# Attention and expert layers on one core: nine of sixteen head pairs keep their probabilities as fp16 halves, turned by DMA

## The chip, the cores and the metric

The kernel runs on one core of a Trainium2 chip. The metric is the device time of one execution in microseconds (us). The engines are TensorE (PE), VectorE (DVE), ScalarE (ACT), GpSimd (POOL) and SyncE (SP), which here only issues DMAs. Each engine takes its own instructions in the order in which they stand in its queue; semaphores join the queues.

## The reference

Attention with queries averaged in pairs, over 4 batches of 8 heads with 1152 keys of 64 numbers, and then a two-layer network on the joined heads:

```python
q_pool = q.reshape(B, H, S // 2, 2, D).mean(axis=3)      # 576 queries per head
scores = scale * np.matmul(q_pool, k.transpose(0, 1, 3, 2))
scores = scores - np.max(scores, axis=-1, keepdims=True)
attn = np.exp(scores)
attn = attn / (np.sum(attn, axis=-1, keepdims=True) + 1e-09)
attn_out = np.matmul(attn, v)
x = attn_out.transpose(0, 2, 1, 3).reshape(B * S, H * D)  # 2304 x 512
h = x @ w_in                                              # 512 -> 2048
g = np.where(h > 0.0, h, np.exp(np.minimum(h, 0.0)) - 1.0)
return g @ w_out                                          # 2048 -> 512
```

## The kernel before, in words

**Units.** A batch is a unit; its 8 heads are 4 head pairs. A pair has 9 steps: four tiles of 128 queries for each head and one step in which the last 64 queries of both heads share the 128 partitions. So a batch has 36 steps and the program 144.

**A step** (`attention`, from L744): `scores` (L761, L766, L773) makes 128x1152 scores in three PSUM banks, the only buffer `s`, out of fp16 halves of query and key; `biggest` (L779, DVE) scales them into an SBUF buffer `ep` (fp32, four buffers) and takes the extreme of each row; `expo` (L785, ACT) writes the exponentials in place with their sum; `recip` (L790, L791, DVE) makes 1/sum; `norm_pool` (L794, POOL; sometimes L797 on DVE) multiplies `ep` by it. Then PE turns the nine 128x128 blocks of `ep` (L820, fp32, into PSUM `r`, three to a buffer) and ACT (L832) or DVE (L835) copies each three into `pT` (fp32). When both heads of a tile are turned, `pv` (L851) multiplies by the values: 18 fp32 matmuls, one head in the first 64 columns of the array and the other in the last 64, into one `r` buffer, which DVE (L863) or ACT (L860) copies to `x32`.

**Before a pair** (`prep`, from L477): SP loads q, k and v; q and k are scaled by a power of two and split into fp16 halves (L492 and L504 or POOL); two DMA transposes (`qT` L571, nine blocks; `kT` L583, eighteen blocks) and three small copies on SP make the operands of `scores`. v stays fp32.

**The network** (`experts`, from L874): for each batch, in two groups of 256 and 320 tokens, 16 first-layer tasks (M1, L949; 24 matmuls of 256 columns or 12 of 320) with activation work on ACT, POOL and DVE (L963 to L1002), and the second layer (M2, L1021) in tasks of 12 matmuls of 512 columns. The last 64 tokens of a batch take 48 matmuls in column halves. Weights are decoded, scaled and split at the start (L645 to L700).

**The order** is set when the program is built. `Plan.run` (L114) plays the program through with a duration for every task and gives an engine, whenever it is free, the ready task with the smallest key whose buffers are free. Keys come from `CFG` (L19) and the position of a step. `weave` (L153) puts the transposes of a step between the matmuls of an M1 or M2 task, one for one.

Of the kernel before, what the change touches and what calls it, by code (L numbers as in the profile page):

```python
# [19 lines left out]
    LOADS=-114467, WI0=33877, WIT=9245, WO0=755935, WOT=6543, T0=2082, T1=1393, M0=16194,  # L20
    M1=49670, KS=15309, KM=4108, KE=81609, KH=27848, KL=992, KV=-2143, KN=220, KX=-18520,
    KO=-10657, PEN=-570, W0L=-16875, WIN=726, PD=18136, KS0=34876, KM0=13622, KE0=132045,
    KH0=40116, KL0=31322, KV0=2811, KX0=-445, PLM0=0, NS0=36, PLM=0, M2=10343, DP=0, FK=0,
    PENW=-3339, PENH=-2500, FL=2000, PH0=2, PH=1, KT=-33611, KT0=390, LV=16680, HW=3136,
    PENN=1577, PENT=23, PLP=1, WLP=1, HIP=0, PA=-2820, PB=-5460,
)

# [21 lines left out]
class Task:  # L49
    def __init__(self, eng, dur, key, emit, after, bufs):  # L50
        self.eng, self.dur, self.key, self.emit = eng, dur, key, emit
        self.ways = {eng: (dur, emit)}
        self.after = [a for a in after if a is not None]
        self.bufs = bufs
        self.pen = None
        self.parts, self.thin, self.guests, self.modes = None, None, [], ("full", "full")
        self.kids, self.left, self.ready, self.end = [], 0, 0.0, None


class Plan:  # L60
# [5 lines left out]
    SWITCH, THIN = 94.0, 58.0  # L66
# [11 lines left out]
    def add(self, eng, dur, key, emit, after=(), bufs=(), ways=(), modes=None, parts=None, thin=None):  # L78
# [6 lines left out]
        t.parts, t.thin = parts, thin  # L85
        t.n = len(self.tasks)
        self.tasks.append(t)
        return t
# [25 lines left out]
    def run(self):  # L114
# [38 lines left out]
        def weave(t, need):  # L153
            hold = {x for x, _ in need}
            host, guests = (None, [(t, need)]) if t.thin else ((t, need), [])
            if host is None:
                for key, _, h in wait["PE"]:
                    if key > t.key + CFG["HW"]:
                        break
                    if h.parts:  # L160
                        got = self._slots_for(h, hold)
                        if got is not None:
                            host = (h, got)
                            hold |= {x for x, _ in got}
                            break
            if host is None:
                return t, need, []
            for key, _, g in wait["PE"]:
                if len(guests) >= len(host[0].parts) // 4:
                    break  # L170
                if g.thin and g is not t:
                    got = self._slots_for(g, hold)
                    if got is not None:
                        guests.append((g, got))
                        hold |= {x for x, _ in got}
            return (*host, guests)

        while done < len(self.tasks):
# [5 lines left out]
            while again:  # L184
                again = False
                for e in engines:
# [23 lines left out]
                    guests = []  # L210
                    if t.parts or t.thin:
                        t, need, guests = weave(t, need)
# [11 lines left out]
                    slow = 1.0 / self.COLD if cold else 1.0  # L224
                    for i, (g, got) in enumerate(guests):
                        self._take(got)
                        gone(g)
                        g.start = now
                        t.guests.append(g)
                        rest[e] += 3 * self.THIN  # L230
                        heapq.heappush(landing, (now + slow * 3 * (i + 1) * (self.THIN + t.dur / len(t.parts)), g.n, g))
                        done += 1
# [44 lines left out]
    def emit(self):  # L277
        for t in self.run():
            for o in [t, *t.guests]:
                for b in o.bufs:  # L280
                    if b.ap is None:
                        ap = self.make[b.tag](b.slot)
                        b.ap = ap if b.tag == b.tags[0] else self.lend[b.tags[0], b.tag](ap)
            if not t.guests:
                t.emit()
                continue
            thin = [f for g in t.guests for f in g.thin]
            for i, f in enumerate(t.parts):
                if i < len(thin):
                    thin[i]()  # L290
                f()
# [3 lines left out]
def attention_moe_kernel(  # L295
# [30 lines left out]
    pool("v32", 3, [128, 2, NCH, D], F32)  # L326
# [4 lines left out]
    pool("sm", 4, [128, 14], F32)  # L331
    pool("nm", 5, [128, 4], F32)
# [5 lines left out]
    pool("us", 3, [128, 16], F32)  # L338
# [3 lines left out]
    pool("tmp", 5, [128, 512], F32)  # L342
    plan.pool("wm", 1, lambda j: None)
    pool("xr", 1, [128, 8], F32)
# [59 lines left out]
    for u in units:  # L404
# [3 lines left out]
        for p in range(NP):  # L408
            pr = Rec()
            pr.u, pr.p, pr.i, pr.t0 = u, p, len(pairs), None  # L410
            pr.steps = []
# [25 lines left out]
    wk = sb.tile([128, 64], F32, name="wk")  # L437
    iwi, cwi, mf, nwi = (wk[:, j * NG:(j + 1) * NG] for j in range(4))
    mo = wk[:, 32:48]
    ck, so_w, wt = wk[:, 48:49], wk[:, 49:50], wk[:, 50:60]  # L440
# [16 lines left out]
    def across(src, n, key, after, bufs, take):  # L457
# [6 lines left out]
        def most():  # L464
            nc.vector.tensor_reduce(xr.ap[0:n, 0:1], xp.ap[0:n, 0:128], axis=AX.X, op=ALU.max)
            nc.vector.tensor_scalar(xr.ap[0:n, 4:4 + n], ident[0:n, 0:n], xr.ap[0:n, 0:1], None, op0=ALU.mult)

        def back():
            nc.tensor.matmul(xp.ap[:, 256:256 + n], ones[0:n].to_broadcast([n, 128]), xr.ap[0:n, 4:4 + n], start=True, stop=True)  # L469
# [7 lines left out]
    def prep(pr, t0, t1):  # L477
# [74 lines left out]
        nsum = 2  # L552
# [5 lines left out]
        sums.append(plan.add("ACT", act(1152) + 90.0, key[1], absum(k_h, k_s, 1), [tk], [kn, k32, sm]))  # L558

        def up(top):  # L560
# [4 lines left out]
            ts(nc.vector, a[:, 12:13], a[:, 0:1], a[:, 1:2], -1.0 / (2.0 * float(D) ** 0.5))  # L565

# [23 lines left out]
        kl = halves(1152, key[6], key[7], k_h, k_l, k_s, 1, [sc], [kn, k32, sm])  # L590
# [153 lines left out]
    def attention(st):  # L744
# [39 lines left out]
        def expo():  # L784
            nc.scalar.activation(  # L785
                out=e_(), in_=e_(), func=AF.Exp, bias=nm.ap[:, 0:1], scale=-1.0, accum_out=nm.ap[:, 2:3],
            )

        def recip():
            nc.vector.tensor_scalar(nm.ap[:, 3:4], nm.ap[:, 2:3], 1e-9, None, op0=ALU.add)  # L790
            nc.vector.reciprocal(nm.ap[:, 3:4], nm.ap[:, 3:4])  # L791

        def norm_pool():
            nc.gpsimd.tensor_scalar(e_(), e_(), nm.ap[:, 3:4], 1.0, op0=ALU.mult, op1=ALU.mult)  # L794

        def norm_dve():
            nc.vector.tensor_scalar(e_(), e_(), nm.ap[:, 3:4], None, op0=ALU.mult)  # L797

        def norm_act():
            nc.scalar.activation(out=e_(), in_=e_(), func=AF.Copy, scale=nm.ap[:, 3:4])  # L800
# [7 lines left out]
        th = plan.add("POOL", pol(S), t0 - K("KH", u), norm_pool, [tr], [ep, nm],  # L808
                      [("DVE", Port(760.0), norm_dve), ("ACT", act(S), norm_act)])
        th.pen = CFG["PENN"]  # L810

# [4 lines left out]
        for j in range(0, NCH, 3):  # L816
            tp = plan.buf("r")

            def one(c, j=j, tp=tp):
                nc.tensor.transpose(tp.ap[:, c * 128:(c + 1) * 128], e_()[:, (j + c) * 128:(j + c + 1) * 128], ident)  # L820

            thin = [lambda c=c, one=one: one(c) for c in range(3)]

            def turn(thin=thin):
                for f in thin:
                    f()

            def dst(j):
                return pT.ap[:, st.h or 0, j:j + 3].rearrange("p c s -> p (c s)")

            def out_act(j=j, tp=tp):
                nc.scalar.activation(out=dst(j), in_=tp.ap[:, 0:384], func=AF.Copy)  # L832

            def out_dve(j=j, tp=tp):
                nc.vector.tensor_copy(dst(j), tp.ap[:, 0:384])  # L835

            tt = plan.add("PE", 335.0, t0 - K("KT", u) + j, turn, [th], [ep, tp, pT], thin=thin)
            tq = plan.add("ACT", 410.0, t0 - K("KL", u) + j, out_act, [tt], [tp, pT], [("DVE", 480.0, out_dve)])
            tq.pen = CFG["PENT"]
            pr.pt.append(tq)  # L840
# [3 lines left out]
        x = plan.buf("r")  # L844

        def pv():
            for c in range(NCH):
                for h in range(2):
# [3 lines left out]
                        x.ap[64 * h:64 * h + 64, 0:n], pr.v32.ap[:, h, order[c]], p,  # L852
                        start=(c == 0), stop=(c == NCH - 1), skip_group_check=True,
                    )

# [3 lines left out]
        def xa():  # L859
            nc.scalar.activation(out=xdst(), in_=x.ap[:, 0:n], func=AF.Copy)  # L860

        def xb():
            nc.vector.tensor_copy(xdst(), x.ap[:, 0:n])  # L863

        tp = plan.add("PE", 18 * (2.0 * n / 2.4 + 2.5), t0 + K("KV", u), pv,
                      list(pr.pt) + pr.vdone, [x, pT, pr.v32], modes=("col", "col"))
        u.xdone[0 if st.t < 2 else 1].append(plan.add("DVE", 230.0, t0 + K("KV", u) - K("KX", u), xb, [tp], [x, u.x32],
# [6 lines left out]
    def experts(u, gi, t0, t1):  # L874
# [60 lines left out]
        if True:  # L935
# [3 lines left out]
            for g in range(NG):  # L939
                for f0 in range(0, 2, per):  # L940
# [15 lines left out]
                    p1 = [lambda f=f, i=i, m1=m1: m1(f, i) for f in range(per) for i in range(3 * KD)]  # L956

                    def m1_all(p1=p1):
# [133 lines left out]
```

## Time and profile before

| | us |
|---|---|
| median of 3 runs | 927.88 (924.21 to 932.52) |
| profiled execution, its own time | 928.17 |
| its span on the core | 926.4 |
| PE busy in the span | 855.7 |
| DVE, ACT, POOL busy | 598.2, 589.2, 390.6 |

The sum of the prediction is made against the profiled execution, 928.2 us, of which the span is 926.4 and 1.8 lies around it. A busy PE is counted from the start of a matmul to its modelled end, and matmuls overlap; so what one matmul costs is read from the distance between starts, or from the chain of work, not from its mean duration.

### The profile page before, as it was taken

To read this page: it belongs to the slowest core of one execution; us is meant where nothing else is said; L and a number is where in the kernel's file an instruction comes from. 1 tells how busy PE (TensorE), PEld (TensorE's weight loads), DVE (VectorE), ACT (ScalarE), POOL (GpSimd) and SP (SyncE) were. 2 spreads that over 40 slices of the span, in tenths; PEclk is the share of its full clock that TensorE was granted. 3 is DMA by queue.
4 is the path that set the end of the run, shared out by engine and by line. 5 is a ranking of instruction groups with operands and counts; after the bars stand their busy time and mean duration, and the time that the engine had idled before them with its cause. 6 is when DMAs were issued, how large, how long until landed. Compare 5 with 4: busy or idle time off the path is not lost.

```text
span 926.4 us, 19421 instructions
## 1 busy us (share of the span) xinstructions
PE 855.7 (92%) x7731; PEld 611.8 (66%) x7731; DVE 598.2 (65%) x1325; ACT 589.2 (64%) x1114; POOL 390.6 (42%) x387
## 2 busy tenths in 40 slices
PE   1268888899999999999999999999999999999997
PEld 0146656687577767776677766777677767777563
DVE  7898889998848765654477656654477646642350
ACT  4457888877757855756577755756578655553460
POOL 3455356378637742433255523343155523332120
PEclk9999999999999999999999999999999999999999
DMA  8963585600404520342151430323160200000000
GB/s 307 231 170 69 158 198 172 174 2 27 109 30 106 123 88 13 70 77 69 41 115 48 89 89 1 71 62 75 49 116 27 59 13 1 13 2 1 29 1 29
DMA packets 97691, 72.30 MB, mean 78 GB/s; under 512 B 59456, under 2 KB 77888, under 8 KB 97600
## 3 DMA queue, kind: packets, MB, share of 16 engines
q1 hardware_dynamic: 97600, 71.06, 30.7%
q8 instruction: 61, 1.00, 0.4%
q14 instruction: 30, 0.25, 0.1%
HBM read 45.09 MB, written 4.72 MB: 54 GB/s over the span
## 4 chain that ended last, share of the span: by engine, by line
PE 76%; DVE 12%; DMA 5%; ACT 3%; issue 2%; POOL 1%; SPq 1%; ACTq 0%; DVEq 0%; POOLq 0%
PE r L949 18%; PE r L1021 17%; PE r L820 14%; PE r L851 14%; PE s L761 7%; PE s L773 4%; DVE ep L779 3%; DMA kT<-kn 3%; DMA qT<-qn 2%; DVE tmp L646 1%; DVE g L649 1%; DVE tmp L645 1%; ACT ep L785 1%; PE s L766 1%; PE r L469 1%
## 5 line engine op out<-in xcount | busy, mean ns | idle before, releaser
L794 POOL TENSOR_SCALAR ep<-ep,nm 128x1152 f32<-128x1152 f32 x139 | 178.7, 1286 | 286.7 <-DVE nm L791 181.1
L820 PE MATMUL r<-ident,ep 128*128 128x128 f32 x1296 | 273.9, 282 | 6.0 <-ACT x L860 1.7
L779 DVE TENSOR_SCALAR_CACHE_REDUCE ep<-s,sm 128x1152 f32<-128x1152 f32 x144 | 203.6, 1414 | 76.9 <-PE r L820 47.0
L949 PE MATMUL r<-x,wi 128*128 128x256 f16 (+1 forms) x1536 | 242.0, 286 | 1.7 <-ACT x L860 1.6
L832 ACT ACTIVATE pT<-r 128x384 f32<-128x384 f32 x334 | 153.8, 489 | 121.2 <-PE r L820 119.3
L785 ACT ACTIVATE ep<-ep,nm 128x1152 f32<-128x1152 f32 x144 | 180.4, 1252 | 66.3 <-DVE ep L779 64.7
L820 PEld LDWEIGHTS r<-ident,ep 128*128 128x128 f32 x1296 | 166.5, 142 | 48.8 <-issue 30.0
L1021 PE MATMUL r<-wo,g 128*128 128x512 f16 (+1 forms) x792 | 180.5, 380 | 0.0
L949 PEld LDWEIGHTS <-wi 128*128 128x128 f16 x1536 | 153.0, 100 | 24.7 <-issue 0.8
L851 PE MATMUL r<-pT,v 128*64 128x128 f32 (+1 forms) x2880 | 160.0, 265 | 1.5 <-ACT pT L832 1.5
L851 PEld LDWEIGHTS r<-pT,v 128*64 128x64 f32 x2880 | 142.6, 137 | 20.4 <-issue 12.1
L761 PE MATMUL s<-kT,qT 128*128 128x512 f16 (+2 forms) x480 | 97.2, 334 | 17.6 <-DVE ep L779 16.8
L1021 PEld LDWEIGHTS <-g 128*128 128x128 f16 (+1 forms) x792 | 69.5, 102 | 62.7 <-issue 1.8
L971 POOL TENSOR_SCALAR tmp<-tmp,us 128x320 f32<-128x320 f32 (+1 forms) x96 | 60.5, 632 | 114.6 <-ACT tmp L966 111.5
L976 DVE SCALAR_TENSOR_TENSOR tmp<-r,wk,tmp 128x320 f32<-128x320 f32 (+1 forms) x96 | 58.2, 612 | 43.4 <-POOL tmp L971 43.0
L761 PEld LDWEIGHTS <-qT 128*128 128x128 f16 (+1 forms) x480 | 39.6, 101 | 54.7 <-issue 27.7
L963 ACT ACTIVATE tmp<-r 128x320 f32<-128x320 f32 (+1 forms) x96 | 46.5, 485 | 36.3 <-PE r L949 31.8
L835 DVE COPY pT<-r 128x384 f32<-128x384 f32 x98 | 53.7, 553 | 19.9 <-PE r L820 19.0
L966 ACT ACTIVATE tmp<-tmp,us 128x320 f32<-128x320 f32 (+1 forms) x96 | 58.6, 612 | 2.0
L773 PE MATMUL s<-kT,qT 64*128 64x512 f16 (+1 forms) x320 | 57.8, 398 | 0.0
L790 DVE TENSOR_SCALAR nm<-nm 128x1 f32<-128x1 f32 x144 | 21.4, 149 | 46.7 <-ACT ep L785 45.8
L1002 DVE TENSOR_TENSOR g<-tmp,g 128x320 f16<-128x320 f32 (+1 forms) x56 | 33.5, 604 | 19.7 <-ACT g L990 14.9
(111 smaller groups left out, 787.1 us busy)
## 6 DMA issues: line engine op xcount, KB each, us to landing
k<-in_k_dram SPq DMA_DIRECT2D x16, 576.0 KB, 4.7
v<-in_v_dram SPq DMA_DIRECT2D x16, 576.0 KB, 3.9
q<-in_q_dram SPq DMA_DIRECT2D x32, 256.0 KB, 3.3
qT<-qT SPq DMA_DIRECT2D x48, 144.0 KB, 2.9
g<-in_moe_w_in_dram SPq DMA_DIRECT2D x13, 512.0 KB, 5.2
g<-in_moe_w_out_dram SPq DMA_DIRECT2D x13, 512.0 KB, 4.3
out_dram<-tmp SPq DMA_DIRECT2D x16, 256.0 KB, 2.0
h<-in_moe_w_in_dram SPq DMA_DIRECT2D x3, 512.0 KB, 3.8
```

The lines of the kernel that those rows point to most:

```text
L761: nc.tensor.matmul(s.ap[rows, c, 0:n], pr.qT.ap[:, 0, j, rows], keys[h][c], start=True, stop=False, skip_group_check=True,)
L773: nc.tensor.matmul(s.ap[rows, c, 0:512], pr.qT.ap[r, 1, j, rows], keys[h][c][r], start=False, stop=True, skip_group_check=True,)
L779: nc.vector.tensor_scalar(e_(), s.ap.rearrange("p a b -> p (a b)")[:, 0:S], pr.sm.ap[:, 12:13], None, op0=ALU.mult, op1=ALU.min, accum_out ...
L785: nc.scalar.activation(out=e_(), in_=e_(), func=AF.Exp, bias=nm.ap[:, 0:1], scale=-1.0, accum_out=nm.ap[:, 2:3],)
L794: nc.gpsimd.tensor_scalar(e_(), e_(), nm.ap[:, 3:4], 1.0, op0=ALU.mult, op1=ALU.mult)
L820: nc.tensor.transpose(tp.ap[:, c * 128:(c + 1) * 128], e_()[:, (j + c) * 128:(j + c + 1) * 128], ident)
L832: nc.scalar.activation(out=dst(j), in_=tp.ap[:, 0:384], func=AF.Copy)
L851: nc.tensor.matmul(x.ap[64 * h:64 * h + 64, 0:n], pr.v32.ap[:, h, order[c]], p, start=(c == 0), stop=(c == NCH - 1), skip_group_check=True,)
L949: nc.tensor.matmul(hp.ap[:, f * n:(f + 1) * n], w_in16[g][:, a, c, (f0 + f) * 128:(f0 + f + 1) * 128], x16.ap[:, e, c, g0:g0 + n], start=( ...
L966: nc.scalar.activation(out=en.ap[:, :m], in_=en.ap[:, :m], func=AF.Exp, scale=us.ap[:, 8 + g:9 + g])
L971: nc.gpsimd.tensor_scalar(en.ap[:, :m], en.ap[:, :m], -1.0, us.ap[:, 5:6], op0=ALU.add, op1=ALU.mult)
L1021: nc.tensor.matmul(op.ap[r0:r0 + tn, :], gt[qd].ap[:, a, fi, o:o + tn], w_out16(f // 2)[:, e, f % 2, :], start=(i < 128 // tn), stop=(i >= ...
```

## The change

A table `SPLIT` marks nine head pairs, three in each of the batches 1 to 3; batch 0 stays as it was. For a marked pair v is split into two fp16 halves as well (`v16`), and its 81 steps go another way after `recip`: ACT or POOL writes the fp16 high half of the normalized probabilities into a new buffer `hb` (two of them), DVE writes the low half over `ep` (L793), and two DMA transposes on SP's queue (L799) turn both into `pT`. The values are multiplied in three terms (high x high, high x low, low x high) with 54 fp16 matmuls in column halves (L862), and the copy to `x32` takes the scale back. `weave` goes: the transposes that stay stand together. All keys of `CFG` are new. To make room, `v32` goes from 3 to 2 buffers, `tmp` from 5 to 4, `sm` from 4 to 3, `us` from 3 to 2, and `nm` and `xr` become columns of `wk`.

```diff
-    LOADS=-114467, WI0=33877, WIT=9245, WO0=755935, WOT=6543, T0=2082, T1=1393, M0=16194,
+    LOADS=-28648, WI0=-4682, WIT=8948, WO0=1686424, WOT=1874, T0=2082, T1=500, M0=16259,
...
+SPLIT = ("ffff", "ssfs", "ssfs", "ssfs")
...
-        def weave(t, need):
...
-    pool("v32", 3, [128, 2, NCH, D], F32)
+    pool("v32", 2, [128, 2, NCH, D], F32)
+    pool("v16", 1, [128, 2, NCH, 2, D], F16)
+    pool("hb", 2, [128, S], F16)
...
-    pool("sm", 4, [128, 14], F32)
-    pool("nm", 5, [128, 4], F32)
+    pool("sm", 3, [128, 14], F32)
+    plan.pool("nm", 5, lambda j: wk[:, 61 + 2 * j:63 + 2 * j])
...
+        if pr.split:
+            v16 = pr.v16 = plan.buf("v16")
+            v_s, v_h, v_l = (lambda: v32.ap), (lambda: v16.ap[:, :, :, 0]), (lambda: v16.ap[:, :, :, 1])
+            sums.append(plan.add("ACT", act(1152) + 90.0, key[2], absum(k_h, v_s, 2), [tv, sums[1]], [kn, v32, sm]))
...
-        pr.vdone = [tv]
+        pr.vdone = [halves(1152, key[11], key[12], v_h, v_l, v_s, 2, [sc], [v16, v32, sm])] if pr.split else [tv]
...
+        if pr.split:
+            hb = plan.buf("hb")
+            e16 = lambda: e_().bitcast(F16)[:, 0:S]
...
+            def phi():
+                nc.gpsimd.tensor_scalar(hb.ap, e_(), nm.ap[:, 1:2], 1.0, op0=ALU.mult, op1=ALU.mult)
+
+            def phi_act():
+                nc.scalar.activation(out=hb.ap, in_=e_(), func=AF.Copy, scale=nm.ap[:, 1:2])
+
+            def plo():
+                nc.vector.scalar_tensor_tensor(
+                    out=e16(), in0=e_(), scalar=nm.ap[:, 1:2], in1=hb.ap, op0=ALU.mult, op1=ALU.subtract
+                )
+
+            def ptr(j):
+                def f():
+                    nc.sync.dma_start_transpose(
+                        out=p16(j).rearrange("p (c s) -> p c s", c=NCH), in_=e16() if j else hb.ap
+                    )
+                return f
...
+            pr.pt.append(plan.add("DMA", Move(1400.0, 1100.0, True), t0 - CFG["KC"], ptr(0), [th], [hb, pT]))
+            pr.pt.append(plan.add("DMA", Move(1400.0, 1100.0, True), t0 - CFG["KC"], ptr(1), [tl], [ep, pT]))
...
+        def pv_split():
+            for j, (a, e) in enumerate(((0, 0), (0, 1), (1, 0))):
+                for c in range(NCH):
+                    for h in range(2):
...
+                        nc.tensor.matmul(
+                            half(h), pr.v16.ap[:, h, order[c], e], p,
+                            start=(j + c == 0), stop=(j == 2 and c == NCH - 1), skip_group_check=True,
+                        )
```

On PE before, in batch 2, the transposes of a step (L820, from `ep` into `r`) stand one for one between the matmuls of an M1 task (L949), and the fp32 product with the values (L851) follows:

```order
L820 MATMUL r1_5350<-ident_70,ep2_5043 128x128
L949 LDWEIGHTS wi0_61
L949 MATMUL r0_5348<-x160_4344,wi0_61 128x320
...
L949 MATMUL r0_5348<-x160_4344,wi0_61 128x320
L851 MATMUL r1_5384<-pT1_5152,v322_3869 64x128 x18
```

On PE after, at about the same place in batch 2, an M2 task (L1035) is followed by the fp16 product with the values of a marked pair (L862; 54 matmuls, each with a weight load of its own) and then by scores (L727):

```order
L1035 LDWEIGHTS g0_4873
L1035 MATMUL r0_5468<-wo2_1476,g0_4873 128x512
L862 LDWEIGHTS v160_5093
L862 MATMUL r2_5566<-pT0_5226,v160_5093 64x128
...
L862 MATMUL r2_5566<-pT0_5226,v160_5093 64x128
L727 LDWEIGHTS qT0_4520
L727 MATMUL s0_5623<-kT0_4495,qT0_4520 64x512
```

Nothing of the marked pair's probabilities passes PE any more before this product.

On DVE before, there, a step's row extreme (L779) stands among copies of transposes (L835) and joins of the network (L976):

```order
L779 TENSOR_SCALAR ep3_5465,nm1_5464<-s0_5412,sm2_3721 128x1152
L835 COPY pT0_5352<-r4_5469 128x384
L976 SCALAR_TENSOR_TENSOR tmp0_5488<-r0_5429,wk_69,tmp0_5488 128x320
L790 TENSOR_SCALAR nm1_5464<-nm1_5464 128x1
L791 RECIPROCAL nm1_5464<-nm1_5464 128x1
```

On DVE after, low halves (L793) of four steps stand ahead of the next row extreme (L745), whose buffer `ep0` is the one that the first of them wrote:

```order
L793 SCALAR_TENSOR_TENSOR ep0_5095<-ep0_5095,wk_69,hb0_5331 128x1152
L990 SCALAR_TENSOR_TENSOR tmp1_5385<-r4_5360,wk_69,tmp1_5385 128x320
L793 SCALAR_TENSOR_TENSOR ep2_5272<-ep2_5272,wk_69,hb1_5375 128x1152
L793 SCALAR_TENSOR_TENSOR ep3_5379<-ep3_5379,wk_69,hb0_5526 128x1152
L793 SCALAR_TENSOR_TENSOR ep1_5466<-ep1_5466,wk_69,hb1_5546 128x1152
L745 TENSOR_SCALAR ep0_5564,wk_69<-s0_5491,sm0_4070 128x1152
```

The row extreme now stands behind a low half and behind its transfer, which frees `ep0`.

On SP's queue after, there, high and low halves (L799, from `hb` and `ep` into `pT`) stand between the transposes and copies of a pair's operands (L537, L543, L546); before, it held no transposes but two for each pair:

```order
L537 DMA_TRANSPOSE qT0_5779<-qn0_5262 128x9x128
L1061 DMA out_0_dram<-tmp0_5668 128x512
L799 DMA_TRANSPOSE pT0_5859<-hb0_5772 128x9x128
L543 DMA qT0_5779<-qT0_5779 64x1152 x2
L799 DMA_TRANSPOSE pT0_5859<-ep1_5744 128x9x128
L799 DMA_TRANSPOSE pT0_5859<-hb1_5790 128x9x128
L546 DMA qT0_5779<-qT0_5779 64x1152
L799 DMA_TRANSPOSE pT0_5859<-ep3_5774 128x9x128
```

One queue serves loads, outputs, operand transposes and the 162 new ones, in this order.

## Rows read from the trace of the kernel before

**Rows 1.** The page: busy time of each engine; PE and DVE in 40 slices.

```profile
span 926.4 us, 19421 instructions
PE 855.7 (92%) x7731; PEld 611.8 (66%) x7731; DVE 598.2 (65%) x1325; ACT 589.2 (64%) x1114; POOL 390.6 (42%) x387
...
PE   1268888899999999999999999999999999999997
...
DVE  7898889998848765654477656654477646642350
```

**Rows 2.** The page: the chain that ended last, by engine and by line.

```profile
PE 76%; DVE 12%; DMA 5%; ACT 3%; issue 2%; POOL 1%; SPq 1%; ACTq 0%; DVEq 0%; POOLq 0%
PE r L949 18%; PE r L1021 17%; PE r L820 14%; PE r L851 14%; PE s L761 7%; PE s L773 4%; DVE ep L779 3%; DMA kT<-kn 3%; DMA qT<-qn 2%; DVE tmp L646 1%; DVE g L649 1%; DVE tmp L645 1%; ACT ep L785 1%; PE s L766 1%; PE r L469 1%
```

**Rows 3.** Busy time by window, cut where a batch's first L779 stands; batches 0 to 2.

```profile
core 0: us, PE busy (x) PEld busy (x) DVE busy (x) ACT busy (x) POOL busy (x), PEclk, DMA share, GB/s
0.00:198.00 198.00, 137.30 (x1321) 99.75 (x1322) 172.64 (x384) 141.36 (x288) 94.58 (x78) 0.99 0.65 173
198.00:406.00 208.00, 205.81 (x1872) 150.43 (x1870) 145.98 (x314) 143.42 (x263) 117.00 (x112) 1.00 0.28 66
406.00:617.00 211.00, 209.59 (x1928) 151.76 (x1927) 128.21 (x294) 136.10 (x252) 83.22 (x86) 1.00 0.28 66
```

**Rows 4.** The same view for three other windows.

```profile
60.00:182.00 122.00, 107.36 (x1117) 78.98 (x1116) 108.48 (x254) 100.85 (x210) 57.69 (x44) 0.99 0.59 154
198.00:820.00 622.00, 616.98 (x5670) 448.16 (x5668) 393.11 (x876) 407.07 (x749) 276.48 (x279) 1.00 0.25 59
...
182.00:240.00 58.00, 56.99 (x517) 42.36 (x517) 52.99 (x101) 45.30 (x84) 43.12 (x39) 1.00 0.13 33
```

**Rows 5.** The chain in order of time (start, us, what): transposes woven and alone.

```profile
423.12 0.11 PE r L820
423.23 0.21 PE r L1021
...
185.64 1.13 PE r L820 x9
```

**Rows 6.** The same chain: products with the values; a pair of column halves.

```profile
353.22 2.12 PE r L851 x36
...
493.69 1.20 PE r L851 x36
...
190.08 0.06 PE s L766 x2
```

**Rows 7.** Groups by line and shape: us in all, mean ns | idle before.

```profile
L785 ACT ACTIVATE ep<-ep,nm 128x1152 f32<-128x1152 f32 x144 | 180.4, 1252 | 66.3 <-DVE ep L779 64.7
L794 POOL TENSOR_SCALAR ep<-ep,nm 128x1152 f32<-128x1152 f32 x139 | 178.7, 1286 | 286.7 <-DVE nm L791 181.1 <-PE r L820 27.5 <-ACT tmp L1039 10.3
L832 ACT ACTIVATE pT<-r 128x384 f32<-128x384 f32 x334 | 153.8, 489 | 121.2 <-PE r L820 119.3
L835 DVE COPY pT<-r 128x384 f32<-128x384 f32 x98 | 53.7, 553 | 19.9 <-PE r L820 19.0
L976 DVE SCALAR_TENSOR_TENSOR tmp<-r,wk,tmp 128x320 f32<-128x320 f32 x64 | 34.3, 544 | 17.1 <-POOL tmp L971 16.7
L976 DVE SCALAR_TENSOR_TENSOR tmp<-r,wk,tmp 128x512 f32<-128x512 f32 x32 | 23.9, 747 | 26.3 <-POOL tmp L971 26.3
```

**Rows 8.** Source lines on DVE and SP: duration ns min/median/max; landing us.

```profile
L504 DVE SCALAR_TENSOR_TENSOR kn<-k,sm,kn x14: 810/832/1831, 408.9 to 717.8; 128x576 f16<-128x576 f32 x14
...
L571 SPq DMA_TRANSPOSE qT<-qn x16: 1283/1846/2481, 24.4 to 729.6; - x16
...
DMA to landing us min/median/max: 3.4/3.8/6.9
...
L583 SPq DMA_TRANSPOSE kT<-kn x16: 2492/4068/7399, 28.3 to 731.0; - x16
```

**Rows 9.** SP's queue in order of time: a plain issue.

```profile
409.33 0.51 SPq L529 DMA_DIRECT2D q<-in_q_dram  x1
```

More of the change, by code (lines that the diff above doesn't have):

```diff
@@ L151, in gone @@
                 wait[o].remove((t.key, t.n, t))
-        def weave(t, need):
[L154 to L176, printed above, removed]
         while done < len(self.tasks):
@@ L278, in emit @@
         for t in self.run():
[L279 to L291, printed above, removed]
+            for b in t.bufs:
+                if b.ap is None:
+                    ap = self.make[b.tag](b.slot)
+                    b.ap = ap if b.tag == b.tags[0] else self.lend[b.tags[0], b.tag](ap)
+            t.emit()
 @with_exitstack
@@ L815, in attention, with one, turn, dst @@
         pT = pr.pT
[L816 to L840, printed above, removed]
+        if pr.split:
+            hb = plan.buf("hb")
+            e16 = lambda: e_().bitcast(F16)[:, 0:S]
+            p16 = lambda j: pT.ap.bitcast(F16).rearrange("p h c s -> p (h c s)")[:, 2 * S * (st.h or 0) + j * S:][:, :S]
+            def phi():
[12 more added lines that the diff above has]
+                return f
+            hw = [("ACT", act(S), phi_act), ("POOL", pol(S), phi)]
+            th = plan.add(*hw[0][:2], t0 - CFG["KA"], hw[0][2], [tr], [ep, nm, hb], hw[1:])
+            tl = plan.add("DVE", dve(S), t0 - CFG["KB"], plo, [th], [ep, nm, hb])
+            pr.pt.append(plan.add("DMA", Move(1400.0, 1100.0, True), t0 - CFG["KC"], ptr(0), [th], [hb, pT]))
+            pr.pt.append(plan.add("DMA", Move(1400.0, 1100.0, True), t0 - CFG["KC"], ptr(1), [tl], [ep, pT]))
+        else:
+            th = plan.add("POOL", pol(S), t0 - K("KH", u), norm_pool, [tr], [ep, nm],
+                          [("DVE", Port(760.0), norm_dve), ("ACT", act(S), norm_act)])
+            th.pen = CFG["PENN"]
+            for j in range(0, NCH, 3):
+                tp = plan.buf("r")
+                def one(c, j=j, tp=tp):
+                    nc.tensor.transpose(tp.ap[:, c * 128:(c + 1) * 128], e_()[:, (j + c) * 128:(j + c + 1) * 128], ident)
+                def turn(one=one):
+                    for c in range(3):
+                        one(c)
+                def dst(j):
+                    return pT.ap[:, st.h or 0, j:j + 3].rearrange("p c s -> p (c s)")
+                def out_act(j=j, tp=tp):
+                    nc.scalar.activation(out=dst(j), in_=tp.ap[:, 0:384], func=AF.Copy)
+                def out_dve(j=j, tp=tp):
+                    nc.vector.tensor_copy(dst(j), tp.ap[:, 0:384])
+                tt = plan.add("PE", 335.0, t0 - K("KT", u) + j, turn, [th], [ep, tp, pT])
+                tq = plan.add("ACT", 410.0, t0 - K("KL", u) + j, out_act, [tt], [tp, pT], [("DVE", 480.0, out_dve)])
+                tq.pen = CFG["PENT"]
+                pr.pt.append(tq)
@@ L844, in attention, with half @@
         x = plan.buf("r")
+        def half(h):
+            return x.ap[64 * h:64 * h + 64, 0:n]
         def pv():
```

105 lines of the change are left out of this document (50 added, 55 removed).

## The prediction

> **What bounds the kernel now.** I read the page's busy shares and slices first, then the chain that ended last, then the busy time by window and at last single lines. The page shows one engine far ahead: PE is busy 92% of the span, DVE 65%, ACT 64%, and PE's slices are at nine tenths from the ninth on while DVE's fall from the twelfth on [rows 1]. The chain says the same: 76% of the span is PE, and of the lines on it the transposes (L820) and the products with the values (L851) have 14% each [rows 2]. The windows show where: in batch 0 PE is busy 137.3 of 198 us and DVE 172.6, so there DVE and the loads set the pace; in batches 1 and 2 PE is busy 205.8 of 208 and 209.6 of 211 us, DVE 146.0 and 128.2 [rows 3]. Over 198 to 820 PE is busy 99.2% (617.0 of 622), DVE 63%, ACT 65%, POOL 44%, at a granted clock of 1.00 [rows 4]. All marked steps lie after batch 0, so what PE saves is saved where PE is the bound, until another engine or queue takes its place.
>
> **PE's terms.** *Transposes.* A marked step loses nine of them; 81 steps make 729. Woven, a transpose holds the chain 0.11 us and the matmul beside it 0.21 [rows 5], so 729 x 0.11 = 80 us go. Of the transposes that stay, batch 0's mostly stand alone already; 27 unmarked steps of later batches lose the weaving, at 0.126 each alone (1.13 for nine) [rows 5]: 243 x 0.016 = +4 us.
>
> *Products with the values.* Nine pairs have 36 whole tiles and nine half ones. A whole fp32 tile takes 2.12 us [rows 6]. The fp16 form needs 54 matmuls of 128 columns, in 27 pairs of column halves. The trace has such a pair in the scores of the shared step: two matmuls of 128 columns in two column halves hold the chain 0.06 us [rows 6]. So 27 x 0.06 = 1.62 us, 0.50 less, and 36 x 0.50 = 18 us go. The bound above is the weight loads: in a half fp32 tile 36 loads and matmuls take 1.20 us, 0.033 each [rows 6]; at that rate 54 take 1.80, and 11.5 us go. A half tile lies between 27 x 0.033 = 0.9 and 1.62 against 1.20: zero, within 3 us either way.
>
> By the Trainium skill (TensorEngine Tiling (Array Packing), Restrictions) column tiling disables the fast weight load, and by its page TensorE: Matmul & The Clock Gate, LDWEIGHTS, a load takes its columns divided by 1.2 in ns, 53 for 64 columns. By that, with loads one after another, a tile would take 2.9 us and the tiles would cost 28 us more instead of 18 less. The trace shows 0.033 us for a load and its matmul [rows 6], so it does not agree for fp32 halves; for 54 fp16 loads on end no run here shows it.
>
> PE's sum: -80 + 4 - 18 = -94. From the profiled execution's 928.2 (0.3 us above the median of the runs, so without a correction) that gives 834 us, if PE stays the bound as it was.
>
> **What the others get.** Between 198 and 820 lie 107 of the 108 steps of batches 1 to 3, in both orders, and 79 marked ones after. PE's 622 us there become about 528.
>
> *DVE* loses the copies (L835, 0.548 each, 53.7 for 98; some 79 of them here, -43) and gains 79 low halves. A scalar-tensor-tensor takes 0.544 us for 320 elements and 0.747 for 512 [rows 7], 1.06 ns an element: 1.42 for 1152, so +112. Six of the nine low halves of v also stand on DVE, +8. Some smaller work moves to ACT, POOL or into batch 0; I leave it out, to DVE's disfavour. 393 + 77 = 470 of 528, 89%. The bound above is contention: the same instruction on half keys has a median of 0.83 us and a maximum of 1.83 [rows 8]; a third more on the low halves would be 507, 96%.
>
> *ACT* loses about 156 copies (L832, 0.46 each, 153.8 for 334), -72, and gains 42 of the 81 high halves at 1.25 (the exponential on the same shape [rows 7]), +53, and v's sum and high half, about 1.25 each for nine pairs, +22. 407 + 3 = 410, 78%. *POOL* loses some 82 of its 107 normalizations and takes 37 high halves, at 1.29 [rows 7]: -58. These two have room.
>
> *SP.* 156 of the 162 new transposes stand in this window. One of nine blocks holds SP's queue 1.28 to 2.48 us, median 1.85 [rows 8]: 200 to 387, 289 at the median. Before, 11 operand pairs (1.85 + 4.07 [rows 8]) and about 106 plain issues at 0.51 [rows 9] make 65 + 54. In all 408 of 528, 77%.
>
> **The new waits.** Before, `ep` was free for the next row extreme when PE had turned it; now when the low half's transfer has landed, 3.4 to 6.9 us after its issue, median 3.8 [rows 8]. Behind a waiting L745 stand the joins and reciprocals on DVE, and PE's next scores wait for it, since `s` is one buffer. A step lasts 1.4 (row extreme, taken as long as a low half) + 1.25 (exponential) + 1.25 (high half) + 1.4 (low half) + 3.8 = 9.1 us without queueing, where steps come every 528/107 = 4.9 us and four `ep` buffers give 19.7: some 10 us are left for sums, reciprocals and queues. Two `hb` buffers give 9.8 us, against 1.25 + 3.8 for the transfer. So no buffer forces a stall by itself; it takes queues that come late together.
>
> What that costs the trace bounds on both sides. In 182 to 240 DVE is busy 53.0 of 58 us (91%), ACT 78%, POOL 74%, and PE still 57.0 (98.3%); in 60 to 182 DVE is at 89%, ACT 83%, and PE only 107.4 of 122 (88%) [rows 4]. The first has network matmuls in PE's queue to fill gaps, the second none (the first L949 runs at 182); the new order has them in batches 1 to 3, so it is nearer the first. By the first PE loses 0.9% more than before, 5 us; by the second 617 - 94 = 523 at 88% takes 594, 66 us more than 528. I take +10. In batch 0 the steps are the same 36; copies go from DVE to ACT and all is reordered: 0, within 12 us either way.
>
> **Sum.** 834 + 10 = 844 us. About 1%, 9 us, is what a measurement of this kernel can tell from no change.
>
> **Rivals.**
> *Another engine sets the pace.* DVE with contention, or DVE and SP late in turn, take PE to the 88% of 60 to 182: 834 + 66 = 900 us, or, short of that, 869 to 900. For it: 89 to 96% on DVE and 77% on SP at once, and low halves in rows of four ahead of a row extreme. Against: 182 to 240 stood it.
> *The 54 weight loads do not overlap.* If a load and its matmul take the 0.059 us of the fp32 tile (2.12 / 36 [rows 6]), a tile takes 3.2 us and a half tile the same: 36 x 1.07 + 9 x 2.0 = +57 in place of -18, so 844 + 75 = 919 us, about the bound of what can be told. Against: the 0.033 rows.
> *Slower: the new transposes serialize on SP's queue.* SP has 622 - 119 = 503 us in the window before it grows longer than it was; for 156 transposes that is 3.2 us each. From there the kernel is slower. If each has to land before the next is issued, at the least landing of 3.4 us [rows 8], the window takes 119 + 530 = 649, 27 more than before: 955 us. For it: probabilities, operands and loads share one queue that stops at its first unmet wait. Against: a transpose of eighteen blocks holds the queue 2.49 us at best [rows 8], 1.25 for nine, less than any landing, so blocks follow on before the earlier ones have landed.
>
> **How the numbers follow.** Forecast 844, its own range 822 to 868: 0.62. Another engine, 869 to 910: 0.18. Loads that do not overlap: 0.06. Serialized transposes: 0.09. Below 822, if batch 0 gains or the order closes gaps: 0.05. The range 815 to 905 holds the forecast, nearly all of the second case and most of the last, some 0.82. Faster by over 1%: 0.62 + 0.18 + 0.05 and a third of the load case, 0.87; within 1%: 0.04; slower by over 1%: 0.09.
>
> **What would show it.** Right: 567 transposes (L818) left; a whole fp16 tile at 1.5 to 1.8 us on the chain; low halves on DVE at 1.4 to 1.6 us; PE at 97% or more of the windows of batches 1 to 3, which shrink from about 207 to about 178 us; L799 holding SP under 2 us. Wrong: PE under 93% there with row extremes waiting on L799's landings or on low halves; a tile over 2 us; SP busy from end to end.

## The result, and the profile after

The changed kernel takes 863.0 us in the median of four runs, against 927.12 us before: a ratio of 0.9285, interval 0.9202 to 0.9368. One of the four ran at a mean granted TensorE clock of 0.574 and took 1276.9 us; it is left out of the ratio, and the other three have a median of 859.15 (858.18 to 866.84). A second measurement on another occasion gave 861.42 us against 926.26, 0.931 (0.9278 to 0.9343). The forecast was 844 us with a range of 815 to 905: faster, as said, and 15 to 19 us short of it, 17 in the second measurement. What follows explains those 17 us as much as the 66 that went.

The profile shown is that of the second measurement. Its page, by engine and in 40 slices [rows 1]:

```profile
span 860.1 us, 19870 instructions
PE 764.9 (89%) x7812; PEld 505.1 (59%) x7812; DVE 663.5 (77%) x1284; ACT 587.6 (68%) x1046; POOL 419.1 (49%) x387
...
PE   1077988899989898998999999999999999999997
...
DVE  7787798999998896778997898688979766765040
...
PEclk9999998999999998999999999999999999999999
```

PE is still the busiest, with 91 us less work, but its slices are no longer at nine from end to end, and DVE's do not fall in the second half as they did. The busy time by window, cut where the first row extreme (L745) of the second, third and fourth batch and the last of all stand [rows 3, 4]:

```profile
core 0: us, PE busy (x) PEld busy (x) DVE busy (x) ACT busy (x) POOL busy (x), PEclk, DMA share, GB/s
0.00:217.70 217.70, 152.85 (x1491) 112.50 (x1491) 182.57 (x400) 161.22 (x333) 98.14 (x84) 0.98 0.57 160
217.70:392.70 175.00, 161.79 (x1655) 99.99 (x1654) 147.15 (x270) 125.02 (x210) 107.06 (x96) 0.96 0.82 156
392.70:576.50 183.80, 177.74 (x1967) 117.49 (x1964) 153.59 (x283) 132.47 (x218) 99.70 (x94) 0.99 0.86 164
576.50:749.80 173.30, 167.58 (x1859) 108.09 (x1858) 139.78 (x258) 127.79 (x211) 85.47 (x79) 1.00 0.76 139
...
217.70:749.80 532.10, 507.11 (x5473) 325.57 (x5472) 440.51 (x809) 385.29 (x639) 292.23 (x267) 0.98 0.81 153
```

The windows of batches 1 to 3 shrink from about 207 to 175, 184 and 173 us. Batch 1 begins 19 us later than before (217.7 against 198): PE has 15.5 us more work ahead of that cut, 152.85 against 137.30, and 4.2 us more idle time. Of the work 8.7 us are matmuls of the first layer (L964, 17.6 us; L949 before, 8.9) and most of the rest products with the values and transposes that the new order does earlier. So the shorter windows are in part work that stands elsewhere now. Over the three batches PE is busy 95.3% (507.1 of 532.1), where it was 99.2% [rows 4], and the granted clock is 0.98 instead of 1.00. In four stretches of these batches, 17 us in all, the clock is at the lower of its two levels (1.2 GHz instead of 2.4). Just ahead of each of them PE had stood idle for 1.9 to 3.3 us in sum. The first of the four, and the time before it:

```profile
235.00:241.60 6.60, 3.26 (x19) 1.54 (x17) 6.46 (x15) 6.25 (x8) 6.01 (x6) 1.00 1.12 194
241.60:245.00 3.40, 3.40 (x57) 2.98 (x56) 3.37 (x7) 3.40 (x6) 3.36 (x3) 0.50 1.20 200
```

The chain in order of time has the new product [rows 6] and what stays of the transposes:

```profile
741.36 1.63 PE r L862 x54
...
743.96 0.49 PE r L818 x3
...
761.01 2.48 PE r L862 x108
```

A whole tile takes 1.63 us; the 108 matmuls are a whole and a half tile, so a half one takes 0.85. What PE waited for in batches 1 to 3 (engine, line and what it waited for: us in total, times, longest):

```profile
PE s L727 <- DVE ep L745: 18.8, 20, 3.0
PE r L964 <- ACT x L871: 1.4, 1, 1.4
```

Of the 25 us that PE idles there, 18.8 are scores that wait for DVE's row extreme to free `s`. Before, the same wait took 1.0 us in batches 1 to 3:

```profile
PE s L761 <- DVE ep L779: 1.0, 2, 0.8
```

The lines of the new operations (duration ns min/median/max) and of SP's transposes [rows 8]:

```profile
L793 DVE SCALAR_TENSOR_TENSOR ep<-ep,wk,hb x81: 1397/1415/2382, 226.5 to 757.2; 128x1152 f16<-128x1152 f32 x81
...
L799 SPq DMA_TRANSPOSE pT<-hb x81: 1242/1339/3304, 223.1 to 757.2; - x81
L799 SPq DMA_TRANSPOSE pT<-ep x81: 1279/1347/2955, 228.0 to 758.7; - x81
...
DMA to landing us min/median/max: 3.2/3.6/6.5
```

Low halves have a median of 1.42 us and a mean of 1.53 (123.8 us for 81). A transpose holds SP 1.34 us. Summed over SP's issues between 217.7 and 749.8 (178 transposes, 281.6 us; 106 plain ones, 60.3) SP is busy 342 of 532 us, 64%.

### The profile page after: what moved, and what is told of

Its sections match the earlier page's. It is cut to its first block, busy times and chain, and to the rows that moved or that the text cites. A ratio compares the mean times of both kernels' runs of the same rounds, so it can differ in the third digit from the quotient of the medians.

```text
span 1275.1 us, 19870 instructions
## 1 busy us (share of the span) xinstructions
PE 1222.0 (96%) x7812; PEld 673.5 (53%) x7812; DVE 651.4 (51%) x1284; ACT 602.4 (47%) x1046; POOL 397.9 (31%) x387
## 3 DMA queue, kind: packets, MB, share of 16 engines
q1 hardware_dynamic: 289408, 118.85, 43.7%
## 4 chain that ended last, share of the span: by engine, by line
PE 93%; DVE 4%; DMA 1%; issue 1%; ACT 1%; SPq 0%; POOL 0%; DVEq 0%; POOLq 0%; ACTq 0%
PE r L964 26%; PE r L1035 26%; PE s L727 9%; PE r L862 8%; PE r L850 8%; PE r L818 8%; PE s L739 4%; PE s L732 1%; PE r L429 1%; DVE tmp L612 1%; DVE ep L745 1%; DVE g L615 0%; DVE tmp L611 0%; DMA g<-in_moe_w_in_dram 0%; PE r L422 0%
## 5 line engine op out<-in xcount | busy, mean ns | idle before, releaser
L964 PE MATMUL r<-x,wi 128*128 128x256 f16 (+1 forms) x1536 | 337.8, 410 | 0.3 <-ACT x L871 0.3
L745 DVE TENSOR_SCALAR_CACHE_REDUCE ep<-s,sm 128x1152 f32<-128x1152 f32 x144 | 203.8, 1415 | 224.2 <-PE s L739 195.3
L1035 PE MATMUL r<-wo,g 128*128 128x512 f16 (+1 forms) x864 | 301.5, 579 | 0.0
L964 PEld LDWEIGHTS <-wi 128*128 128x128 f16 x1536 | 195.1, 129 | 129.3 <-issue 10.7
L751 ACT ACTIVATE ep<-ep,wk 128x1152 f32<-128x1152 f32 x144 | 180.0, 1250 | 148.8 <-DVE ep L745 100.2
L1035 PEld LDWEIGHTS <-g 128*128 128x128 f16 (+1 forms) x864 | 99.2, 133 | 173.3 <-issue 168.2
L727 PE MATMUL s<-kT,qT 128*128 128x512 f16 (+2 forms) x480 | 147.2, 472 | 8.5 <-DVE ep L745 7.9
L763 POOL TENSOR_SCALAR ep<-ep,wk 128x1152 f32<-128x1152 f32 x59 | 74.1, 1256 | 233.4 <-DVE wk L760 175.5
L828 ACT ACTIVATE pT<-r 128x384 f32<-128x384 f32 x189 | 90.6, 489 | 87.4 <-PE r L818 75.1
L793 DVE SCALAR_TENSOR_TENSOR ep<-ep,wk,hb 128x1152 f16<-128x1152 f32 x81 | 120.8, 1496 | 8.2 <-ACT hb L790 4.7
L818 PE MATMUL r<-ident,ep 128*128 128x128 f32 x567 | 119.9, 379 | 0.9 <-ACT x L871 0.5
L862 PE MATMUL r<-pT,v 128*64 128x128 f16 (+1 forms) x2430 | 111.2, 276 | 0.0
L862 PEld LDWEIGHTS <-v 128*64 128x64 f16 x2430 | 100.3, 140 | 17.2 <-issue 14.9
L818 PEld LDWEIGHTS r<-ident,ep 128*128 128x128 f32 x567 | 81.1, 162 | 32.5 <-issue 14.4
L990 DVE SCALAR_TENSOR_TENSOR tmp<-r,wk,tmp 128x320 f32<-128x320 f32 (+1 forms) x96 | 57.1, 609 | 79.1 <-POOL tmp L985 79.1
L727 PEld LDWEIGHTS <-qT 128*128 128x128 f16 (+1 forms) x480 | 48.5, 123 | 80.1 <-issue 67.0
```

Source lines behind the costliest of these rows:

```text
L727: nc.tensor.matmul(s.ap[rows, c, 0:n], pr.qT.ap[:, 0, j, rows], keys[h][c], start=True, stop=False, skip_group_check=True,)
L745: nc.vector.tensor_scalar(e_(), s.ap.rearrange("p a b -> p (a b)")[:, 0:S], pr.sm.ap[:, 12:13], None, op0=ALU.mult, op1=ALU.min, accum_out ...
L751: nc.scalar.activation(out=e_(), in_=e_(), func=AF.Exp, bias=nm.ap[:, 0:1], scale=-1.0, accum_out=nm.ap[:, 1:2],)
L763: nc.gpsimd.tensor_scalar(e_(), e_(), nm.ap[:, 1:2], 1.0, op0=ALU.mult, op1=ALU.mult)
L793: nc.vector.scalar_tensor_tensor(out=e16(), in0=e_(), scalar=nm.ap[:, 1:2], in1=hb.ap, op0=ALU.mult, op1=ALU.subtract)
L862: nc.tensor.matmul(half(h), pr.v16.ap[:, h, order[c], e], p, start=(j + c == 0), stop=(j == 2 and c == NCH - 1), skip_group_check=True,)
```

## The experiments

Theory A: PE idles for time on SP's queue and for landings. Theory B: it idles for DVE's own work. Theory C: PE's work and clock set the time. Every kernel keeps the order of the changed kernel unless said otherwise; times are medians, and "SP busy" is the same sum as above.

**The change measured again.** No edit.

> The changed kernel as it is, for a profile at full clock: about 860 us. Theory A (PE is still the bound in batches 1 to 3, and what the prediction missed is PE time): PE busy 97% or more of those windows, a whole fp16 tile near 1.6 us on the chain. Theory B (new waits for DVE or for SP's queue): PE under 95% there, with scores waiting for row extremes, or products waiting for the new transposes.

Measured: 861.42 us (860.19 to 865.78). The profile above is from here: PE under 97% and scores behind row extremes, as the expectation's second theory has it.

**Before without weaving.** In `Plan.run` of the kernel before:

```diff
-                    if t.parts or t.thin:
-                        t, need, guests = weave(t, need)
```

> The kernel before with the weaving alone taken out; transposes of a step stand together, the rest of the order is played through anew with the same keys. Some 108 steps of batches 1 to 3 were woven: at 0.126 us instead of 0.11 for each of 972 transposes that is +15 us, 943 us. If weaving mattered for the waits of the copies behind it, more: over 950.

Measured: 947.64 us, 1.0231 (1.0199 to 1.0262) of before, 21 us more. The rate of 0.016 us for each of the 972 transposes of batches 1 to 3 gives 16. PE's busy time grew by 8.3 (864.0 against 855.7) and its idle time by 11 (span 945.9 against 926.4). So less than half of the 21 us is PE's own work; why it idles more without the weaving was not isolated. For the 243 transposes that lost it in the change, a quarter of the 972, that is 4 us by the rate and 5 by the measurement, where the sum had 4.

**No transposes of low halves.** `ptr(1)` issues nothing, and the low x high term reads the high half:

```diff
+                    if j:
+                        return
-                        p = p[:, h, a, c] if st.h is not None else ...
+                        p = p[:, h, 0, c] if st.h is not None else ...
```

> The changed kernel in its own order, with the 81 transposes of the low halves not issued; the product with the values reads the high half in the low x high term too, so the low half of the probabilities is left out of the result. DVE still computes the low halves, PE still does 54 matmuls a tile. Theory A (the 20 us that PE idles in batches 1 to 3 come from SP's queue and from ep being freed only when the low half's transfer has landed): 10 to 20 us less than the changed kernel's 861, so 841 to 851, with PE at 98% of the batch windows and fewer waits of scores for row extremes than 31 us. Theory B (they come from DVE's own work, the low halves standing ahead of row extremes): 0 to 5 us less, 856 to 861. Theory C (PE's work and its clock set the time, the waits only move about): the same as the changed kernel within 4 us.

Measured: 850.65 us (849.19 to 851.32), ratio 0.9165 (0.9142 to 0.9188): 11 us less, in theory A's range, though PE is at 96.8% and not at 98. Batches 1 to 3, and PE's wait for row extremes in them:

```profile
218.30:739.50 521.20, 504.64 (x5473) 325.50 (x5472) 438.72 (x808) 385.86 (x640) 294.02 (x267) 0.99 0.56 113
```

```profile
PE s L727 <- DVE ep L745: 12.6, 11, 2.6
```

**No low halves at all.** As above, and `plo` (L793) does nothing:

```diff
             def plo():
+                return
```

> As the run without the low halves' transposes, and DVE's 81 low halves are not computed either, which takes 120 us of DVE's busy time away; the low half of the probabilities is left out of the result. PE's work is that of the changed kernel. Theory A: as the run without the transposes within 4 us, so 841 to 851. Theory B: 15 to 25 us less than the changed kernel, 836 to 846, PE at 98% of the batch windows. Theory C: within 4 us of 861 once more.

Measured: 840.91 us (838.31 to 842.26), ratio 0.9055 (0.9023 to 0.9086): 10 us less again, 20 in all. So A and B each have a part, and theory C falls.

```profile
220.20:729.40 509.20, 497.84 (x5455) 320.69 (x5454) 323.62 (x730) 385.00 (x640) 251.87 (x267) 1.00 0.57 115
```

```profile
PE s L727 <- DVE ep L745: 8.7, 10, 2.2
```

With DVE at 64% of the batches instead of 83%, PE is at 97.8%. Its own work is unchanged, yet it counts 9 us less of it there (497.8 against 507.1), at a granted clock of 1.00 instead of 0.98: the lower level holds for 3.4 us of these batches instead of 17. An estimate from these two: 13.6 us less at half speed are some 7 of the 9 us. So by these rows PE's idle time cost twice, once while it idled and once by the clock after it.

DVE's low halves also slow POOL. With the same 267 instructions in these batches POOL is busy 294.0 us where DVE computes them (the run before this one) and 251.9 where it does not. One line shows it, over the whole program in the kernel before, the changed kernel and this run:

```profile
L971 POOL TENSOR_SCALAR tmp<-tmp,us 128x320 f32<-128x320 f32 (+1 forms) x96 | 60.5, 632 | 114.6 <-ACT tmp L966 111.5
L985 POOL TENSOR_SCALAR tmp<-tmp,us 128x320 f32<-128x320 f32 (+1 forms) x96 | 77.3, 807 | 65.3 <-ACT tmp L980 64.9
L988 POOL TENSOR_SCALAR tmp<-tmp,us 128x320 f32<-128x320 f32 (+1 forms) x96 | 64.5, 672 | 88.2 <-ACT tmp L983 86.4
```

What of the 10 us is DVE's time and what POOL's was not separated.

**One term of three.** `pv_split` with the high x high term alone:

```diff
-            for j, (a, e) in enumerate(((0, 0), (0, 1), (1, 0))):
+            for j, (a, e) in enumerate(((0, 0),)):
```

> The changed kernel in its own order, with the high x high term of the split product alone: 18 matmuls a tile in place of 54, so the two small terms are left out of the result. DVE, ACT, POOL and SP keep all their work. If PE sets the pace (theory C): 36 whole tiles lose 1.08 us each (1.62 to 0.54) and 9 half ones about 0.6, 44 us in all, so 817 to 825. If DVE and the transfers set the pace as soon as PE is a little faster (theories A and B): 0 to 20 us less, 841 to 861, with PE's idle time in batches 1 to 3 grown from 25 to 45 us or more.

Measured: 854.11 us (848.71 to 855.49), ratio 0.9194 (0.9157 to 0.923): 7 us where PE's sum was 44.

```profile
216.10:738.80 522.70, 474.35 (x3961) 287.82 (x3961) 440.75 (x808) 384.79 (x639) 291.65 (x267) 0.97 0.81 156
```

In the profiled execution, the fastest of the four (848.71), PE's busy time in batches 1 to 3 falls by 33 us and the batches by 9; the idle time doubles, from 25 to 48 us. PE no longer sets the pace by itself.

**One term, and no low halves.** Both edits:

> No low halves on DVE, no transposes of them, and the high x high term alone in the split product: the low half and two of three terms are left out of the result. One term alone took 7 us off the changed kernel, no low halves alone 21. Theory of a joint bound (PE is the limit as soon as DVE lets it be: 44 us less PE work is worth little while DVE's row extremes stand behind low halves, and all of it without them): 44 less PE work come off the 841 of the run without low halves, nearly in full, 800 to 812 us. Rival (something else is the limit close behind, such as the chain scores, row extreme, scores through the one buffer s, or ACT): 7 to 15 us off, 826 to 834 us, with PE at 93% or less of batches 1 to 3.

Measured: 826.61 us (823.64 to 827.58), ratio 0.8916 (0.8885 to 0.8947): 14 us below the run without low halves, not 30 to 41. The rival's range holds. PE is at 93.2%, and scores wait for row extremes 38.5 us over the span while row extremes wait for scores 46.1: this points to the loop through the one `s` buffer as the limit close behind, which no run tested by itself.

```profile
217.00:716.00 499.00, 465.09 (x3948) 284.56 (x3946) 322.64 (x729) 384.32 (x642) 251.30 (x266) 0.99 0.58 117
```

```profile
DVE ep L745 <- PE s L739: 46.1, 48, 3.1
PE s L727 <- DVE ep L745: 38.5, 41, 2.7
```

**What of the transposes costs 11 us.** They read a weight tile, so that `ep` is free after the low half:

```diff
-                        ..., in_=e16() if j else hb.ap
+                        ..., in_=w_in16[0].rearrange("p a c f -> p (a c f)")[:, 0:S] if j else hb.ap
```

> The changed kernel in its own order; the 81 transposes of the low halves stay on SP's queue, at their places and of their size, but read a weight tile that has long been written instead of the low half, so the low half is left out of the result (other numbers stand in its place). DVE still computes the low halves. The transfers no longer wait for DVE's low half and no longer keep ep from the next row extreme. Theory E (the 11 us that went when these transposes were not issued are ep being kept until its transfer has landed): as in that run, 848 to 854 us. Theory Q (they are the load of SP's queue and of the DMA engines, busy 81% of batches 1 to 3 in place of 56%): as the changed kernel, 858 to 864 us.

Measured: 861.56 us (859.81 to 864.86), ratio 0.9307 (0.9277 to 0.9337): nothing gained, as theory Q has it. In the changed kernel DVE waited 4.7 us for these transfers to free `ep` (L745, in batches 1 to 3), here not at all, and the time is the same; so the cost lies in the load and not in `ep`. The same without low halves on DVE (`plo` returns at once):

> The same, and DVE's 81 low halves are not computed (they are left out of the result). DVE has 120 us less to do, SP and the DMA engines have the whole load of the changed kernel. Theory E: as the run with neither low halves nor their transposes, 838 to 844 us. Theory Q, with the two costs in a sum: 849 to 854 us. If DVE's work alone is what the batches wait for, and transfers only through it, again 838 to 844 us, and then the run with DVE's low halves and these transposes tells E from Q.

Measured: 853.44 us (850.38 to 858.7), ratio 0.9221 (0.9179 to 0.9263). So DVE's low halves cost 8 to 10 us with or without the transposes, and the transposes 11 to 13 with or without the low halves: within the spread of the runs, some 3 us, the two add up.

**SP's queue or the DMA engines.** In place of the low transpose, three small plain copies (here the high half is also read for the low x high term), or one large one:

```diff
+                    if j:
+                        for z in (0, 1, 2):
+                            nc.sync.dma_start(out=p16(1)[:, 384 * z:384 * z + 64], in_=...[:, 384 * z:384 * z + 64])
+                        return
```

```diff
+                    if j:
+                        nc.sync.dma_start(out=p16(1), in_=...[:, 0:S])
+                        return
```

> The changed kernel in its own order; in place of each of the 81 transposes of low halves SP issues three plain copies of 128 x 64 numbers from a weight tile that has long been written, and the low x high term reads the high half (the low half is left out of the result). Three plain issues hold SP's queue about 3 x 0.5 = 1.5 us, as long as one transpose (1.35), and move a sixth of the bytes. Theory S (the 12 us of these transposes are time on SP's queue): 858 to 865 us, as with the static transposes (861.6). Theory D (they are load on the DMA engines, which slows every other landing): 848 to 855 us, as without the transposes (850.7), at a DMA share of about 0.6 in batches 1 to 3.

> The same with one plain copy of the whole 128 x 1152 tile in place of each of these transposes: SP's queue is held about 0.5 us, a third of a transpose, and the DMA engines move as many bytes as for the transpose, in larger pieces, so that the DMA share lies somewhere between 0.56 and 0.83 (the low half is left out of the result). Theory S: a third of the 12 us, 852 to 856 us. Theory D: by the DMA share that shows, in proportion between 850.7 (0.56) and 861.6 (0.83).

Measured: 865.04 us (863.64 to 867.3; ratio 0.9333, 0.9309 to 0.9358) with three small copies, 851.3 us (847.69 to 854.48; 0.9194, 0.9165 to 0.9223) with one large. Batches 1 to 3 of the first, with the last two columns the DMA share and GB/s:

```profile
217.70:753.00 535.30, 507.03 (x5445) 324.76 (x5445) 438.10 (x806) 385.68 (x640) 290.28 (x267) 0.98 0.59 117
```

and of the second:

```profile
217.70:739.00 521.30, 504.41 (x5498) 324.86 (x5498) 437.35 (x811) 383.89 (x638) 293.35 (x265) 0.99 0.71 158
```

The kernel with the lower DMA share is the slower one, by 14 us; theory D had 848 to 855 for it, and by its share 857 for the other. SP is busy 370 us in these batches with the small copies and 349 with the static transposes (865 and 862 us), 283 with the large copy and 213 without the transposes (both 851). It is time on SP's queue that costs, theory S; and not in proportion, since between 213 and 283 us nothing shows. A rival is left that the share does not rule out: many small pieces could make the other transfers land later. They do not. The transposes of the high halves land in a median of 3.3 us in the slow kernel (first line, small copies) and 3.5 in the fast one:

```profile
pT<-hb SPq DMA_TRANSPOSE x81, 3.3
pT<-hb SPq DMA_TRANSPOSE x81, 3.5
```

They are issued later. From the end of a high half on ACT or POOL to the issue of its transpose (the writes and the issues of the timeline paired in order) a median of 2.6 us pass with the small copies, 1.8 with the static transposes, 1.1 with the large copy and 0.2 without the transposes.

**Relief for SP, nothing left out.** Loads of q, k and v of batches 1 to 3 (L484, L489, L496) and the stores (L1061) go to another engine's queue, POOL's or ACT's:

```diff
-                nc.sync.dma_start(
+                (nc.gpsimd if u.i else nc.sync).dma_start(
...
-                    nc.sync.dma_start(out=out[r0:r0 + tn, :], in_=ot.ap[0:tn])
+                    nc.gpsimd.dma_start(out=out[r0:r0 + tn, :], in_=ot.ap[0:tn])
```

and the same with `nc.scalar`.

> The changed kernel, whole, with the loads of q, k and v of batches 1 to 3 and the stores of the output on POOL's DMA queue in place of SP's: 73 issues of about 0.55 us, 40 us, leave SP's queue in batches 1 to 3, where it was busy 342 of 532 us (64%) and would be busy 302 (57%), near the 54% of the run with plain copies (851.3). Theory S (time on SP's queue costs the 12 us): 851 to 857 us. Rival (the issues cost the engine that now makes them, or wait there for buffers ahead of its own work): 861 to 880 us, with POOL's waits for hb and ep longer.

> The same loads and stores on ACT's DMA queue. Theory S: 851 to 857 us, if an issue holds ACT 0.1 us or less. Rival: if each holds ACT about as long as it held SP (0.55 us), 40 us more on ACT, which was busy 72% of batches 1 to 3, so 80% now, and exponentials come later: 861 to 875 us.

Measured: 919.58 us on POOL (917.08 to 919.93; ratio 0.9903, 0.9867 to 0.994) and 880.76 on ACT (878.21 to 884.82; 0.9501, 0.9451 to 0.9552), 58 and 19 us worse than the changed kernel, and above every range that was expected of them. Of the first, waits over the span and one line of loads:

```profile
PE s L727 <- DVE ep L745: 53.6, 37, 7.8
...
POOL out_dram L1061 <- ACT tmp L1051: 48.1, 6, 17.5
```

```profile
L484 POOL DMA_DIRECT2D q<-in_q_dram x24: 747/778/980, 122.5 to 721.4; - x24
```

A store that waits up to 17.5 us for its source now holds up the high halves and normalizations behind it on POOL, and an issue takes POOL's own time. On SP the same waits held up only transfers. How the 58 us divide between the two was not tried, nor what makes up the 19 on ACT; so these runs do not test theory S, since they load another engine. No version measured here that computes everything is faster than the changed kernel.

## Why the prediction was right, and where it fell short

*PE's terms held.* 567 transposes are left, and a whole tile takes 1.63 us where 1.62 was forecast. The half tiles, put at zero, gave 0.35 each (1.20 to 0.85), 3 us for nine. PE's busy time fell by 90.8 us (855.7 to 764.9) against a sum of 94. In the run without low halves, at a granted clock of 1.00 in the batches, it fell by 98 (to 757.4): the terms were a little too small, and 7.5 us were given back, most of them to the stretches at the lower clock.

*The weight loads.* 54 loads and matmuls in 1.63 us are 0.030 us each, as the fp32 halves had shown (0.033 [rows 6]). So the case of loads that do not overlap fell. With it fell the estimate of 2.9 us for a tile from the figure of the Trainium skill (TensorE: Matmul & The Clock Gate, LDWEIGHTS): the trace does not agree with one load after another at that rate.

*Other engines.* DVE got 440 us of 470 forecast and POOL 292, not 218. Of the 74 us more, some 40 are POOL's own work going slower beside DVE's low halves (252 without them, with the same instructions), a term that the sum did not have; half of the rest are low halves of the network (45 in these batches, 43.7 us without DVE's; before, L994, 26 with 26.0), which it had left on DVE. ACT got 385 of 410. SP's size was also too high, 342 us instead of 408, because a transpose holds it 1.34 us in the median and not 1.85.

*The step that failed is the +10 for new waits.* PE's idle time grew from 70.7 (926.4 - 855.7) to 95.2 us (860.1 - 764.9), by 24.5: 20.0 in batches 1 to 3 (5.0 to 25.0), 4.2 ahead of them, which the forecast had put at zero within 12. With PE's work 3 us above its sum this is the whole miss: 14.5 + 3.2 = 17.7, and 842.2 + 17.7 = 859.9 for the span (844 less the 1.8 around it). Part of PE's work belongs here too: in the run without low halves it is 4 us below its sum (757.4), and what brings it above is mostly the lower clock behind idle time. The place was named right: scores behind a row extreme that is late on DVE. The size was taken from 182 to 240, where PE stood 91% on DVE at 98.3%; the truth lay between it and the 88% of the other end, at 95.3%. In that window SP's eight issues took 8 of 58 us (14%), against 64% now; the forecast weighed DVE, ACT and POOL there and left SP's queue out. The runs show two parts, 8 to 10 us for low halves on DVE and 11 to 13 for time on SP's queue. Of the two new waits the forecast spoke of, `ep` kept until its transfer lands costs nothing measurable (861.56 with that wait taken out). In the kernels that kept DVE's low halves, all three terms and the loads on SP, the waits for row extremes go with SP's queue, 31 to 34 us over the span where SP is busy 342 to 370 us of the batches and 26 where it is busy 213 or 283; which transfer's lateness carries that to DVE was not isolated.

*The rivals.* Transposes serializing on SP's queue at 3.2 us each did not come: they hold it 1.34 and land in 3.6, so they follow on. "Another engine sets the pace" was put at 869 to 910 and did not set the time, but it stood nearer than the forecast said: 33 us less PE work in the batches are worth 7. Had PE's terms been larger, most of the rest would not have shown.

*The signs.* Of what was to show a right forecast, the 567 transposes, the tile, the low halves (1.42 to 1.53 us) and the hold of SP came; PE at 97% did not. None of the signs of a wrong one came. The windows, 177 us in the mean where 178 was forecast, agree by luck: PE has 110 us less work in batches 1 to 3 and not 94, since 15.5 of it stand ahead of them now, and that made up for the idle time.

## What to carry to other kernels

When work leaves the bounding engine, price what is left by its idle time at the new load of all queues, the DMA queue's included: at 64% of SP, 83% of DVE and one score buffer PE lost 4%, though none of them was full. A DMA issue is worth counting by how long it holds its queue, not by its bytes. And look at what stands behind a transfer before it moves to another queue: moving 40 us of issues off SP cost 19 and 58 us on engines with work to do.

## What was unexpected of the hardware

The DMA engines' share rose from 25% to 81% of batches 1 to 3 without a cost that these runs can tell: 0.71 gave 851.3 us, 0.59 gave 865.0. A transpose of nine blocks took, as an estimate, about 1.8 us of all sixteen engines: (0.81 x 532.1 - 0.56 x 521.2) / 78, for the 78 low ones in these batches. The same load instruction (L484) held SP's queue 0.37 to 0.67 us, and POOL 0.75 to 0.98. And DVE's 81 low halves made the same 267 instructions of POOL 42 us longer (251.9 to 294.0), while DVE's own joins on the same tasks kept their 0.609 us (L990 and L993).
